# An attention kernel's last 64 keys as four 64 by 64 products, with a new order of the work

## The chip, the cores and the metric

One program runs on one core of a Trainium2 chip. The metric is the device time of one execution in microseconds (us). The kernel before has a median of 964.04 us over three runs (960.63 to 966.95). One further execution was taken with the profiler.

## The reference

The program is three layers, one after the other, in float32: an attention with a threshold, a block that adds the real part of a two-dimensional Fourier transform and an MLP (2048 hidden channels), and a block that mixes tokens with two 576 by 576 matrices. The change concerns the first layer alone.

```
batch, n_heads, seq, head_dim = (4, 8, 576, 64)
scores = scale * np.matmul(q, k.transpose(0, 1, 3, 2))
thresh = np.max(scores, axis=-1, keepdims=True) - tau
scores = np.where(scores >= thresh, scores, -1000000000.0)
scores = scores - np.max(scores, axis=-1, keepdims=True)
attn = np.exp(scores)
attn = attn / (np.sum(attn, axis=-1, keepdims=True) + 1e-09)
return np.matmul(attn, v).astype(np.float32)
```

A sequence has 576 = 4 x 128 + 64 tokens. The last 64 keys are what the four full blocks of 128 leave over.

## The kernel before

**The work of the attention.** The 32 heads are taken as 16 pairs `p` (0 to 15); `h` is 0 or 1, the head in its pair. The queries of a head are cut into two halves: half 0 has 256 queries, half 1 has 320. For every pair there are nine tiles of 128 queries. For each tile TensorE makes the scores in one bank pair `ps` (L454, L464, L469, L470), VectorE takes the maximum (`evac`, L478), ScalarE the exponential (`exp`, L483), VectorE multiplies by the mask and sums (`mask`, L494), TensorE transposes the result 128 by 128 (`turn`, L501, and L541 for the keys left over), and ScalarE copies the transposed blocks out of PSUM (`hi`, L510, L548, L550), to `st[h, half]` for the first 512 keys and to `st["r", h]` (tile `pt5`) for the last 64. In `st["r", h]` the queries of half 0 have their last 64 keys in partitions 0 to 63, and those of half 1 have theirs in partitions 64 to 127.

**The product with V** (`pv_ops`, L560, with its matmul at L571) is one operation `("pv", (p, half))` of the planner for each half. It takes a PSUM bank `O`, and for each of five blocks `kt` of 128 rows it issues one matmul for each head: V's block is the 128 by 64 weight, the transposed scores are the 256 or 320 columns that stream, and the heads write partitions 0 to 63 and 64 to 127 of the same bank. In the trace each of these float32 calls is two LDWEIGHTS and two MATMUL, so an operation `pv` is 20 of each. The fifth block holds the last 64 keys: V's block 4 has them in rows 0 to 63 with zeros below, and block 5 has zeros above and the same keys in rows 64 to 127; half 0 uses block 4, and half 1 block 5. Half of the rows of the fifth block are so multiplied by zero.

**After the product** VectorE multiplies each bank `O` by the reciprocal sums `R` into `xT` (L576): `("mu", p)` for half 0, after `pv` of half 0, then `("mul", p)` for half 1, after `pv` of half 1 and after `mu`. The bank is free again after that. GpSimd's first folding of the Fourier transform (`f0`, L675) waits for `mul`.

**The banks.** The tag `O` has four PSUM banks. They serve the transposes `T`, the spread of `R` (L611, L613), the products `O`, and the matmuls of the Fourier transform and the MLP.

**The order** is made when the program is built. Class `Plan` holds all operations with an engine, a cost, a priority, what they come after, and the buffers that they make and use. `schedule` runs a list schedule with these costs; `emit` issues the instructions in that order, so that each engine's order is fixed in the program. A long table `SHIFT` adds a number to the priority of each operation that fits a pattern, as `(('pv', 6), 26.31)`. The work of later layers (normalisation of finished rows, transposes `uT`, hidden layer `h` at L1194, output `acc` at L1214 to L1216, and so on) is in the same plan, so that it fills gaps of the attention.

Of the kernel before, what the change touches and what calls it, by code (L numbers as in the profile page):

```python
# [18 lines left out]
B, H, S, D = 4, 8, 576, 64  # L19
# [248 lines left out]
def attention_and_fft(pl, tc, ident, tb, pss, left, middle, right, qk, vv, cfk, cst, csr, u_d):  # L268
# [156 lines left out]
    def pair(p):  # L425
# [134 lines left out]
        def pv_ops(half, g):  # L560

            loc = {}
            a, n = ((0, 256), (256, 320))[half]
            b, j = divmod(heads(p), 4)

            def mms(e):
                O = loc["O"] = pl.bank([128, 512], f"O{p}_{half}")
                for kt in range(5):
                    for h in range(2):
                        w, x = VR[p][:, h * 6 + (kt if kt < 4 else 4 + half)], st[h, half][:, kt] if kt < 4 else st["r", h][:, :n]  # L570
                        e.matmul(O[64 * h:64 * h + 64, :n], w, x, start=(kt == 0), stop=(kt == 4))  # L571

            def mul(e):
                if p % 4 == 0 and not half:
                    xTs[b] = new("xT", [128, 4, S], f"xT{b}")
                e.tensor_mul(xTs[b][:, j, a:a + n], loc["O"][:, :n], st["R"][:, a:a + n])  # L576

# [4 lines left out]
            pl.op(("pv", k), "PE", 5 * TWO_PASS * n / 256 + 250, pr(g, 3), mms, deps + [("vr", p)], [O],  # L582
                  [("vr", p), ("pt5", p, 0), ("pt5", p, 1), (f"p0{half}", p), (f"p1{half}", p)])
            after = [("pv", k), ("Rc", p, half)] + ([("mu", p)] if half else []) + ([("mul", 4 * b)] if p % 4 else [])
# [385 lines left out]
THREE = 36  # L970
WARM = 7
# [607 lines left out]
class Late:  # L1579
# [180 lines left out]
    (('a6', 12), -9.79), (('a6', 4), -12.89), (('bound',), -9.54), (('bound', 11, 4), -148.11), (('bound', 12), 8.27),  # L1760
    (('bound', 12, 4), -142.12), (('bound', 13, 7), 18.02), (('bound', 13, 8), -21.26), (('bound', 14, 4), -258.91),
    (('bound', 3, 0), -117.73), (('bound', 3, 2), -273.97), (('bound', 6, 5), -179.47), (('bound', 6, 6), -259.98),
# [4 lines left out]
    (('evac', 2, 2), 163.27), (('evac', 3, 8), -187.58), (('evac', None, 3), 39.3), (('exp',), -39.47),  # L1767
    (('exp', 0), -196.98), (('exp', 0, 0), -8.7), (('exp', 0, 3), 56.52), (('exp', 0, 6), 230.59),
    (('exp', 0, 7), 2.61), (('exp', 1), -112.02), (('exp', 1, 5), 26.07), (('exp', 13, 3), 4.13),
    (('exp', 2, 6), 81.45), (('exp', None, 3), -32.63), (('exp', None, 6), -30.61), (('f', 0, 0, 2), -35.3),  # L1770
# [237 lines left out]
```

## Time and profile before

| what | value |
|---|---|
| median of three runs | 964.04 us (960.63 to 966.95) |
| profiled execution, its own time | 962.4 us |
| profiled execution, its span (first to last instruction) | 960.5 us |
| TensorE's matmuls busy | 937.9 us |
| VectorE busy | 626.9 us |
| ScalarE busy | 441.7 us |
| GpSimd busy | 301.9 us |
| granted clock of TensorE | 1.00 throughout |

The page calls TensorE's matmuls PE and its weight loads PEld, VectorE DVE, ScalarE ACT, GpSimd POOL. "Busy" is time in which at least one instruction of the engine is under way. Matmuls overlap in the pipeline, so that the sum of their durations is more than the time that they take; what one costs is read from the distance between starts. Attention fills about the first 330 us; the MLP and the token mixing come after it.

### The profile page before, as it was taken

The page shows a single profiled execution, that of the slowest core. Times are in us where ns is not written, and L with a number is a line of the kernel's source. Part 1 is how long each engine was busy: PE and PEld are TensorE (multiplying, and loading weights), DVE is VectorE, ACT ScalarE, POOL GpSimd, SP SyncE. Part 2 cuts the span into 40 slices and gives each one's busy share as a digit, 9 for nine tenths or more (in the row PEclk, how much of TensorE's full clock was granted, in tenths as well). Part 3 has the DMA queues.
Part 4 walks back from the last instruction along what each step waited for, and adds up shares of the span by engine and source line. Part 5 has one row for each costly group of instructions (what it writes and reads, how often), then busy time and mean ns, then how long its engine had stood idle before and what let it go on. Part 6 is the DMA issues. An engine that isn't in the chain of part 4 may idle for free.

```text
span 960.5 us, 15977 instructions
## 1 busy us (share of the span) xinstructions
PE 937.9 (98%) x5746; PEld 807.1 (84%) x5746; DVE 626.9 (65%) x1225; ACT 441.7 (46%) x835; POOL 301.9 (31%) x468
## 2 busy tenths in 40 slices
PE   8899999999999999999999999999999999999998
PEld 6666788788778788888888888999988899999998
DVE  6777888898898889963553255232257475486832
ACT  6777877787777645530332132011143242253500
POOL 3466656657664643520232032000000021130100
PEclk9999999999999999999999999999999999999999
DMA  6897747765772478645893575241518612213011
GB/s 180 217 218 177 192 122 189 188 187 123 230 188 63 148 221 239 193 132 127 227 291 131 118 218 187 67 86 46 164 30 302 180 41 66 53 56 91 23 51 50
DMA packets 136623, 139.53 MB, mean 145 GB/s; under 512 B 77536, under 2 KB 98720, under 8 KB 136160
## 3 DMA queue, kind: packets, MB, share of 16 engines
q1 hardware_dynamic: 135520, 134.87, 50.9%
q0 software_dynamic: 720, 2.76, 1.1%
q8 instruction: 46, 0.75, 0.3%
q10 hardware_dynamic: 304, 0.87, 0.3%
q14 instruction: 33, 0.27, 0.1%
HBM read 77.34 MB, written 32.05 MB: 114 GB/s over the span
## 4 chain that ended last, share of the span: by engine, by line
PE 80%; DVE 5%; ACT 3%; DMA 2%; issue 1%; SPq 0%; DVEq 0%; POOL 0%
PE h L1194 20%; PE y L1474 12%; PE acc L1216 7%; PE acc L1214 7%; PE acc L1215 7%; PE f L1539 5%; PE th L1351 5%; PE O L571 5%; PE T L501 3%; PE ps L469 2%; PE ps L470 2%; DVE P L494 1%; DVE c L478 1%; ACT P L483 1%; PE ps L464 1%
## 5 line engine op out<-in xcount | busy, mean ns | idle before, releaser
L1194 PE MATMUL h<-uh,w 128*128 128x512 f32 (+1 forms) x640 | 197.5, 370 | 0.1
L1199 ACT ACTIVATE hh<-h 128x512 fp32r<-128x512 f32 (+1 forms) x80 | 44.4, 555 | 222.4 <-PE acc L1215 166.3
L1203 DVE SCALAR_TENSOR_TENSOR hl<-h,hh 128x512 fp32r<-128x512 f32 (+1 forms) x80 | 50.7, 634 | 135.9 <-ACT hh L1199 135.8
L1194 PEld LDWEIGHTS h<-uh,w 128*128 128x128 f32 x640 | 118.8, 188 | 17.3 <-DVE hl L1203 0.2
L494 DVE SCALAR_TENSOR_TENSOR P<-ps,c,P 128x576 f32<-128x576 f32 x144 | 115.1, 813 | 11.7 <-ACT P L483 9.2
L478 DVE TENSOR_REDUCE c<-ps 128x1 f32<-128x576 f32 x144 | 106.1, 750 | 21.1 <-PE ps L470 13.4
L1194 PE MATMUL h<-ul,w 128*128 128x512 f32 (+1 forms) x320 | 118.1, 369 | 0.0
L483 ACT ACTIVATE P<-ps,c 128x576 f32<-128x576 f32 x144 | 105.9, 749 | 22.5 <-DVE c L478 19.1
L1214 PE MATMUL acc<-w,hh 128*128 128x512 f32 x288 | 112.8, 392 | 0.0
L1216 PE MATMUL acc<-w,hl 128*128 128x512 f32 x288 | 112.6, 391 | 0.0
L1215 PE MATMUL acc<-w,hh 128*128 128x512 f32 x288 | 112.4, 390 | 0.0
L1474 PE MATMUL y<-w,z 128*128 128x288 f32 x768 | 106.9, 294 | 0.0
L1474 PEld LDWEIGHTS y<-w,z 128*128 128x128 f32 x768 | 104.0, 188 | 0.9
L501 PE MATMUL T<-ident,P 128*128 128x128 f32 x576 | 83.7, 275 | 4.6 <-DVE P L494 2.0
L510 ACT COPY pt<-T 128x512 f32<-128x512 f32 (+1 forms) x160 | 83.8, 555 | 9.1 <-PE T L501 8.2
L571 PE MATMUL O<-pt,vr 128*64 128x256 f32 (+1 forms) x640 | 84.7, 411 | 0.5 <-ACT R L624 0.5
L469 PE MATMUL ps<-H,L 128*128 128x288 f32 x240 | 75.7, 332 | 3.7 <-DVE P L494 3.0
L501 PEld LDWEIGHTS T<-ident,P 128*128 128x128 f32 x576 | 66.7, 140 | 11.7 <-ACT pt L510 4.5
L571 PEld LDWEIGHTS O<-pt,vr 128*64 128x64 f32 x640 | 43.1, 137 | 31.2 <-issue 3.9
L1194 PEld LDWEIGHTS h<-ul,w 128*128 128x128 f32 x320 | 60.1, 188 | 8.9
L470 PE MATMUL ps<-X,L 128*128 128x288 f32 x240 | 67.0, 295 | 0.0
L1216 PEld LDWEIGHTS acc<-w,hl 128*128 128x128 f32 x288 | 54.1, 188 | 11.8
(358 smaller groups left out, 1678.5 us busy)
## 6 DMA issues: line engine op xcount, KB each, us to landing
raw<-in_qk SPq DMA_DIRECT2D x14, 608.0 KB
vr<-in_vv SPq DMA_DIRECT2D x16, 384.0 KB
w<-w_d SPq DMA_DIRECT2D x6, 992.0 KB
H<-hs SPq DMA_DIRECT2D x30, 160.0 KB
X<-raw SPq DMA_DIRECT2D x30, 160.0 KB
X<-hs SPq DMA_DIRECT2D x30, 160.0 KB
H<-raw SPq DMA_DIRECT2D x30, 160.0 KB
mu<-u_d SPq DMA_DIRECT2D x18, 256.0 KB
```

The lines of the kernel that those rows point to most:

```text
L469: e.matmul(ps[:, half, :HS], L[:, qo:qo + 128], H[:, ko:ko + HS], start=(j == 0), stop=False)
L470: e.matmul(ps[:, half, :HS], L[:, qo:qo + 128], X[:, ko:ko + HS], start=False, stop=(j == n - 1))
L478: e.tensor_reduce(loc["c4"][:, 0:1], loc["ps"][:, :, :HS], axis=AXES.XY, op=ALU.max, negate=True)
L483: e.activation(halves(), loc["ps"][:, :, :HS], AF.Exp, bias=loc["c4"][:, 0:1], scale=1.0)
L494: e.scalar_tensor_tensor(halves(), loc["ps"][:, :, :HS], loc["c4"][:, 1:2], halves(), op0=ALU.is_ge, op1=ALU.mult, accum_out=st["sums"][:, ...
L501: e.transpose(T[:, kt * 128:(kt + 1) * 128], P[:, kt * 128:(kt + 1) * 128], ident[:])
L571: e.matmul(O[64 * h:64 * h + 64, :n], w, x, start=(kt == 0), stop=(kt == 4))
L1194: e.matmul(loc["ps"][:, :n], a, x[:, c, :n], start=(k == 0), stop=(k == 11))
L1214: e.matmul(a, hh[:, q], wh, start=(f == 0), stop=False)
L1215: e.matmul(a, hh[:, q], wl, start=False, stop=False)
L1216: e.matmul(a, hl[:, q], wh, start=False, stop=(f == NF - 1))
L1474: e.matmul(loc["ps"][:, half, :HS], z[:, cs], w, start=(n == 0 and m == 0), stop=(n == 8 and m == 2))
```

## The change

For pairs 4 to 15 (`CORNERS_FROM = 4`) the operation `pv` of each half has only the four full blocks. When half 1 has issued its four, it issues `corners`: four matmuls with 64 rows and 64 weight columns each, two for each half and head, over the 64 partitions that hold the keys, without the zeros. The first two use rows 0 to 63 with output partitions 0 to 63 (half 0, head 0) and rows 64 to 127 with partitions 64 to 127 (half 1, head 1); the next two are head 0 of half 1 and head 1 of half 0. Outputs of half 0 go to the bank of half 0, those of half 1 to the bank of half 1.

From this follow other waits. `pv` of half 0 no longer waits for the copies of the last keys (`hi` with "r"). `pv` of half 1 comes after `pv` of half 0 and uses its bank too. `mu` comes after `pv` of half 1 instead of half 0, so that the bank of half 0 stays taken until then. Pairs 0 to 3 are as before. The planner's costs of `pv` change with it. The branch `MERGED` is off.

The last part of `SHIFT` (about 100 lines of numbers) is replaced by another, so the order of the operations on all engines is a new one.

```diff
+            crossed = p >= CORNERS_FROM
+            both = crossed and MERGED
+            def block(e, kt, half, n):
+                for h in range(2):
+                    w, x = VR[p][:, h * 6 + (kt if kt < 4 else 4 + half)], st[h, half][:, kt] if kt < 4 else st["r", h][:, :n]
+                    e.matmul(st["O", half][64 * h:64 * h + 64, :n], w, x, start=(kt == 0), stop=(kt == 4))
+            def corners(e):
+                for flip in range(2):
+                    for h in range(2):
+                        half = h ^ flip
+                        n, r = (256, 320)[half], slice(64 * half, 64 * half + 64)
+                        e.matmul(st["O", half][64 * h:64 * h + 64, :n], VR[p][r, h * 6 + 4 + half], st["r", h][r, :n], start=False,
+                                 stop=True)
             def mms(e):
-                O = loc["O"] = pl.bank([128, 512], f"O{p}_{half}")
-                for kt in range(5):
-                    for h in range(2):
-                        w, x = VR[p][:, h * 6 + (kt if kt < 4 else 4 + half)], st[h, half][:, kt] if kt < 4 else st["r", h][:, :n]
-                        e.matmul(O[64 * h:64 * h + 64, :n], w, x, start=(kt == 0), stop=(kt == 4))
+                for i in range(2) if both else (half,):
+                    if not both or i:
+                        st["O", i] = pl.bank([128, 512], f"O{p}_{i}")
+                    for kt in range(4 if crossed else 5):
+                        block(e, kt, i, (256, 320)[i])
+                if crossed and half:
+                    corners(e)
...
+            elif crossed and not both:
+                deps = [d for d in deps if half or d[1][1] != "r"]
+                pl.op(("pv", k), "PE", 4 * TWO_PASS * n / 256 + 250 + half * 660, pr(g, 3), mms, deps + [("vr", p)] + [("pv", (p, 0))] * half, [O],
+                      [("vr", p)] + (pts + [("O", (p, 0))] if half else pts[2:]))
+            elif not both:
+                pl.op(("pv", k), "PE", 5 * TWO_PASS * n / 256 + 250, pr(g, 3), mms, deps + [("vr", p)], [O], [("vr", p)] + pts)
-            after = [("pv", k), ("Rc", p, half)] + ([("mu", p)] if half else []) + ([("mul", 4 * b)] if p % 4 else [])
+            after = [("pv", (p, 1) if crossed else k), ("Rc", p, half)] + ([("mu", p)] if half else []) + ([("mul", 4 * b)] if p % 4 else [])
...
+CORNERS_FROM = 4
+MERGED = False
...
-    ((('zh', 2), 10), 46.37), ((('zh', 2, 1),), -1.67), ((('zh', 3),), 30.91), ((('zl', 2, 1), 17), 51.65),
-    (('Rc',), -77.86), (('Rc', 11, 0), -92.43), (('Rc', None, 1), -93.24), (('Re', 0), -6.46), (('Rt',), -3.02),
...
+    (('Rc',), -93.67), (('Rc', None, 1), -46.21), (('Re',), -69.91), (('Rt',), -11.46), (('Rt', 0, 1), 200.1),
...
```

## Rows read from the trace of the kernel before

**Rows 1.** The page: busy us by engine (share of span) x instructions; granted clock in slices

```profile
PE 937.9 (98%) x5746; PEld 807.1 (84%) x5746; DVE 626.9 (65%) x1225; ACT 441.7 (46%) x835; POOL 301.9 (31%) x468
...
PEclk9999999999999999999999999999999999999999
```

**Rows 2.** Windows (A:B, length, busy us with counts by engine, clock, DMA share, GB/s)

```profile
0.00:96.00 96.00, 86.10 (x579) 64.59 (x580) 69.06 (x162) 70.21 (x138) 50.30 (x109) 1.00 0.80 198
96.00:288.00 192.00, 186.31 (x1461) 153.96 (x1461) 170.91 (x406) 151.33 (x317) 120.59 (x230) 1.00 0.68 177
288.00:336.00 48.00, 47.50 (x360) 40.04 (x356) 40.87 (x87) 31.47 (x65) 25.59 (x47) 1.00 0.32 106
336.00:840.00 504.00, 502.45 (x2544) 436.90 (x2544) 272.82 (x409) 150.70 (x236) 91.52 (x74) 1.00 0.52 148
840.00:960.50 120.50, 115.57 (x810) 111.60 (x809) 73.20 (x165) 37.98 (x82) 13.86 (x11) 1.00 0.18 54
```

**Rows 3.** Groups by line: the product with V (busy us, mean ns)

```profile
L571 PE MATMUL O<-pt,vr 128*64 128x256 f32 (+1 forms) x640 | 84.7, 411 | 0.5 <-ACT R L624 0.5
```

**Rows 4.** Timeline (start us, us, engine, line, what, count, [idle before]): V product, pair 9

```profile
200.81 2.38 PE L571 MATMUL O<-pt,vr 128*64 128x256 f32 x20
...
203.12 0.19 PEld L469 LDWEIGHTS ps<-H,L 128*128 128x128 f32 x1 [0.39 <-issue]
...
205.25 2.91 PE L571 MATMUL O<-pt,vr 128*64 128x320 f32 x20
```

**Rows 5.** Timeline, stretches of some 0.1 us in pair 9's half 0: instructions then under way

```profile
200.81 0.44 PE L571 MATMUL O<-pt,vr 128*64 128x256 f32 x2
...
201.08 0.14 PEld L571 LDWEIGHTS O<-pt,vr 128*64 128x64 f32 x2
...
201.29 0.14 PEld L571 LDWEIGHTS O<-pt,vr 128*64 128x64 f32 x2
```

**Rows 6.** Timeline, short stretches in pair 0: its products of 64 by 64

```profile
11.43 0.27 PE L501 MATMUL T<-ident,P 128*128 128x128 f32 x1
...
11.63 0.46 PE L454 MATMUL ps<-x 64*64 64x288 f32 x2
...
11.93 0.14 PEld L454 LDWEIGHTS ps<-x 64*64 64x64 f32 x2
...
12.17 0.14 PEld L454 LDWEIGHTS ps<-x 64*64 64x64 f32 x2
...
12.41 0.41 PE L454 MATMUL ps<-x 64*64 64x288 f32 x2
...
12.75 0.18 PEld L454 LDWEIGHTS ps<-x 64*128 64x128 f32 x1 [0.44 <-issue]
...
13.10 0.19 PEld L454 LDWEIGHTS ps<-x 64*128 64x128 f32 x1
```

**Rows 7.** Timeline, pair 6: transposes, their copies, the product with V, the multiplications

```profile
147.95 0.42 DVE L576 TENSOR_TENSOR xT<-O,R 128x256 f32<-128x256 f32 x1
...
148.44 0.60 PE L501 MATMUL T<-ident,P 128*128 128x128 f32 x4
...
149.08 0.65 ACT L510 COPY pt<-T 128x256 f32<-128x256 f32 x2
...
150.78 2.91 PE L571 MATMUL O<-pt,vr 128*64 128x320 f32 x20
...
153.74 0.49 DVE L576 TENSOR_TENSOR xT<-O,R 128x320 f32<-128x320 f32 x1 [1.64 <-PE O L571]
154.31 0.74 POOL L675 TENSOR_TENSOR gte<-xT 128x256 f32<-128x256 f32 x1 [2.80 <-DVE xT L576]
```

**Rows 8.** Waits of TensorE in 0 to 336 us: total us, times, longest

```profile
PE ps L469 <- DVE P L494: 3.0, 5, 1.3
PE T L501 <- DVE P L494: 2.0, 3, 1.1
PE T L541 <- DVE P L494: 1.8, 2, 1.2
PE ps L464 <- DVE P L494: 1.7, 1, 1.7
PE T L501 <- ACT pt L510: 1.5, 3, 0.8
```

More of the change, by code (lines that the diff above doesn't have):

```diff
@@ L575, in mul @@
                     xTs[b] = new("xT", [128, 4, S], f"xT{b}")
-                e.tensor_mul(xTs[b][:, j, a:a + n], loc["O"][:, :n], st["R"][:, a:a + n])
+                e.tensor_mul(xTs[b][:, j, a:a + n], st["O", half][:, :n], st["R"][:, a:a + n])
             k = (p, half)
@@ L581, in pv_ops @@
             deps = [("hi", (p, i)) for i in idxs] + [("hi", (p, "r", i)) for i in ((0, 1), (0, 1, 2))[half]]
-            pl.op(("pv", k), "PE", 5 * TWO_PASS * n / 256 + 250, pr(g, 3), mms, deps + [("vr", p)], [O],
-                  [("vr", p), ("pt5", p, 0), ("pt5", p, 1), (f"p0{half}", p), (f"p1{half}", p)])
-            after = [("pv", k), ("Rc", p, half)] + ([("mu", p)] if half else []) + ([("mul", 4 * b)] if p % 4 else [])
+            pts = [("pt5", p, 0), ("pt5", p, 1), (f"p0{half}", p), (f"p1{half}", p)]
+            if both and half:
+                deps = sorted(set(deps + [("hi", (p, i)) for i in range(9)]), key=str)
+                pl.op(("ob", p), None, 0, pr(g, 3), hold, deps + [("vr", p)], [("O", (p, 0))])
+                pl.op(("pv", k), "PE", 4 * TWO_PASS * 576 / 256 + 540 + 380, pr(g, 3), mms, [("ob", p)],
+                      [O], [("O", (p, 0)), ("vr", p)] + pts + [(f"p00", p), (f"p10", p)])
+            elif crossed and not both:
[5 more added lines that the diff above has]
+            after = [("pv", (p, 1) if crossed else k), ("Rc", p, half)] + ([("mu", p)] if half else []) + ([("mul", 4 * b)] if p % 4 else [])
             made = [xT] if p % 4 == 0 and not half else []
@@ L1823 @@
-    (('turn', 6, 'r', 2), 30.33), (('turn', 7, 0), 52.88), (('turn', 7, 6), -48.38), (('turn', 8, 1), -6.83),
-    (('turn', 8, 5), -6.33), (('turn', 8, 'r', 0), 53.41), (('turn', 8, 'r', 2), -18.89), (('turn', 9, 3), 36.09),
-    (('turn', 9, 5), 873.6), (('turn', 9, 'r', 2), 5.09), (('turn', None, 0), -10.96), (('turn', None, 3), 1.46),
-    (('turn', None, 6), 1.04), (('turn', None, None, 0), -9.37), (('turn', None, None, 2), 5.29),
[6 rows of a table removed]
[25 rows of a table added]
+    (('a7',), -12.78), (('bound',), -95.59), (('bound', 11), 28.14), (('bound', 11, 7), 57.59), (('bound', 12), 8.27),
@@ new lines @@
+    (('bound', 13, 3), 44.69), (('bound', 2, 0), 65.87), (('bound', 8, 5), 215.69), (('bound', 9, 7), 127.98),
[5 rows of a table added]
+    (('evac',), -178.51), (('evac', 13), 19.4), (('evac', 2, 2), 163.27), (('evac', 3, 8), -187.58),
+    (('evac', None, 2), 18.13), (('exp',), -38.8), (('exp', 0), -207.81), (('exp', 0, 0), -8.7),
+    (('exp', 0, 3), 61.61), (('exp', 0, 6), 371.63), (('exp', 0, 7), 2.61), (('exp', 1), -109.89),
+    (('exp', 1, 5), 9.65), (('exp', 2, 1), 115.23), (('exp', 2, 6), 81.45), (('exp', 3, 1), 106.15),
[26 rows of a table added]
@@ new lines @@
+    (('mask',), -270.06), (('mask', 12, 7), 378.09), (('mix',), 25.77), (('mix', 0), -19.35), (('mix', 0, 3), -16.37),
+    (('mix', 0, 3, (0, 1), 0), -49.31), (('mix', 1, 0, (0, 1), 1), 57.12), (('mix', 1, 1, (0, 1), 0), -48.46),
+    (('mix', 1, 2, (0, 1), 0), 24.31), (('mix', 1, None, (0, 1)), 35.27), (('mix', 2), 8.04), (('mix', 2, 0), 34.55),
+    (('mix', 2, 1, (0, 1), 0), -48.26), (('mix', 2, 3), 10.11), (('mix', 2, 3, (0, 1), 0), -62.26),
+    (('mix', 2, 3, (0, 1), 7), -51.56), (('mix', 2, None, (0, 1)), 0.27), (('mix', 3), -36.8),
@@ new lines @@
+    (('mix', 3, 0, (1,), 0), 10.84), (('mix', 3, 2, (0,), 2), 72.52), (('mix', 3, 3), -25.32),
+    (('mix', 3, 3, (0,), 4), 123.76), (('mix', 3, None, (0,)), -18.45), (('mix', None, 0, (0,)), 16.78),
+    (('mix', None, 1), 17.12), (('mix', None, 2), -4.3), (('mix', None, 3, (0, 1)), -18.42),
+    (('mix', None, None, (0, 1)), -6.92), (('mix', None, None, (0, 1), 7), 16.69), (('n0',), 67.33),
[4 rows of a table added]
+    (('pv', None, 1), -1.05), (('raw', 14), 887.04), (('reload',), -0.55), (('second',), 143.83),
+    (('second', 4, 6), -140.9), (('ta',), 16), (('ta', 0), 126.78), (('ta', 15), 38.24), (('ta', 17), 90.07),
@@ new lines @@
+    (('table',), -55.5), (('th',), -21.67), (('th', 2), 10.47), (('th', 5), 5.29), (('th', 6), -0.27),
+    (('tl', 11), 42.06), (('tl', 4), 12.02), (('turn',), -0.34), (('turn', 0), -18.25), (('turn', 0, 0), -63.36),
+    (('turn', 0, 2), -102.19), (('turn', 0, 4), -57.47), (('turn', 0, 8), -26.78), (('turn', 1, 1), -43.85),
+    (('turn', 1, 2), -36.2), (('turn', 1, 'r'), -36.55), (('turn', 1, 'r', 0), 64.88), (('turn', 10, 1), -4.31),
+    (('turn', 10, 3), 17.42), (('turn', 10, 'r', 0), 57.47), (('turn', 11, 0), 32.88), (('turn', 11, 4), 29.86),
@@ new lines @@
+    (('turn', 11, 7), -12.81), (('turn', 12), -4.13), (('turn', 12, 1), -12.29), (('turn', 12, 2), -11.65),
+    (('turn', 12, 3), -5.86), (('turn', 12, 4), 18.88), (('turn', 13, 1), -6.02), (('turn', 13, 2), -21.03),
+    (('turn', 13, 4), 16.4), (('turn', 14), 5), (('turn', 14, 2), 15.41), (('turn', 14, 4), 86.51),
+    (('turn', 14, 'r', 0), 84.02), (('turn', 14, 'r', 2), -27.4), (('turn', 15), 15.62), (('turn', 15, 1), 23.18),
+    (('turn', 15, 2), -19.98), (('turn', 15, 4), 46.89), (('turn', 15, 5), 14.35), (('turn', 15, 7), 34.76),
@@ new lines @@
+    (('turn', 15, None, 0), 2.69), (('turn', 15, 'r'), -36.16), (('turn', 15, 'r', 0), 76.64), (('turn', 2), -4.2),
+    (('turn', 2, 2), -5.61), (('turn', 2, 4), 22.52), (('turn', 2, 5), -6.85), (('turn', 2, 6), 10.8),
+    (('turn', 2, 7), -12.55), (('turn', 2, 8), -1.75), (('turn', 2, 'r', 1), 28.6), (('turn', 2, 'r', 2), -21.23),
+    (('turn', 3), -4.45), (('turn', 3, 3), -4.8), (('turn', 3, 5), -2.89), (('turn', 3, 6), 11.7),
+    (('turn', 3, 7), -39.86), (('turn', 3, 8), 19.38), (('turn', 4, 0), 37.63), (('turn', 4, 7), 29.21),
@@ new lines @@
+    (('turn', 5), 0.92), (('turn', 5, 4), 19.48), (('turn', 5, 'r', 0), 59.05), (('turn', 6, 0), 29.53),
+    (('turn', 6, 1), -9.5), (('turn', 6, 4), 34.86), (('turn', 6, 'r', 2), 43.41), (('turn', 7), -2.89),
+    (('turn', 7, 'r'), -2.43), (('turn', 7, 'r', 0), 59.27), (('turn', 7, 'r', 2), -22.03), (('turn', 8), -0.66),
+    (('turn', 8, 0), 37.35), (('turn', 8, 2), -0.6), (('turn', 8, 4), 23.81), (('turn', 8, 5), -6.33),
+    (('turn', 8, 'r'), 1.43), (('turn', 8, 'r', 0), 60.36), (('turn', 8, 'r', 2), -17.65), (('turn', 9), 8.16),
@@ L1833 @@
+    (('turn', 9, 0), 25.84), (('turn', 9, 4), 34.61), (('turn', None, 0), -18.09), (('turn', None, 2), 1.31),
+    (('turn', None, 3), 1.74), (('turn', None, 4), -0.9), (('turn', None, 6), -0.35), (('turn', None, 7), -9.28),
+    (('turn', None, None, 0), -11.54), (('turn', None, 'r'), 6.95), (('turn', None, 'r', 0), -5.56),
[4 rows of a table added]
 )
```

32 lines of the change are left out of this document (2 added, 30 removed), and 120 rows, old and new, of the table SHIFT.

## The prediction

> **What bounds the kernel now.** I read the page first. TensorE has a matmul under way for 937.9 of the 960.5 us of the span, at a granted clock of 1.0, so at the upper of its two levels, 2.4 GHz; VectorE is next with 626.9 us [rows 1]. An average can mislead, so the table of windows comes second [rows 2]. From 336 to 840 us TensorE idles 1.6 us in 504. From 840 us on it idles 4.9 us. In the attention it idles 9.9 us before 96 us, 5.7 us from 96 to 288 us and 0.5 us from 288 to 336 us: 16.1 us in all. Pairs 4 to 15, the ones that change, lie in the last two of these stretches. There TensorE is busy for 97 and 99%, VectorE for 170.9 of 192 us (89%) and 40.9 of 48 us (85%). So TensorE bounds the stretch that changes, with VectorE not far behind. Since TensorE hardly idles from there to 840 us, and later layers' work fills gaps of the attention, I take time saved on TensorE in these pairs to arrive at the end one for one, unless it turns into waiting.
>
> Third, the waits of TensorE: the long ones are for VectorE's mask (L494), 8.5 us in the four rows that name it, and for ScalarE's copies, 1.5 us [rows 8]. No row on the product with V is among them. Last, the product itself: 640 matmuls, 84.7 us busy [rows 3]. In pair 9 half 0 takes 2.38 us and half 1 takes 2.91 us [rows 4]; sixteen times both is 84.6 us, so pair 9 stands for all.
>
> **The change, part by part.**
>
> *Removed: the fifth block of both halves.* A call is two matmul instructions, a block two calls, so a block is four of an operation's twenty instructions. In half 0 two matmuls are already under way in the first stretch, and two weight loads go together at 201.08 and again at 201.29: two matmuls run side by side, one for each head, in steps of 0.21 to 0.22 us (the ten steps of 2.38 us with the last one's drain) [rows 4, 5]. I take 0.215 us. Half 1 is 0.53 us longer over ten steps, so its step is 0.053 us longer: 0.27 us. A block is two steps: 0.43 us in half 0 and 0.54 us in half 1, 0.97 us for each pair.
>
> *Added: four products of 64 by 64.* Eight instructions. Two have 256 columns and two have 320, and a product of 320 cannot take less than its own two steps, 0.54 us. No row shows four at once. The nearest are pair 0's products of 64 by 64: two heads, on other rows and other columns, together, a step every 0.24 us (11.93 to 12.17, 12.17 to 12.41) for 288 columns [rows 6]; and the product with V, two heads on the same rows with other columns, together [rows 5]. The new case is two products on the same columns with other rows. Each writes its own bank there (half 0's or half 1's), so nothing that they write is shared. Below: 0.54 us, all four together. Above: 2 x (0.43 + 0.54) = 1.94 us, one after another; two by two it is 4 x 0.27 = 1.08 us. I take 0.54 us, because both kinds of neighbour in the trace run together, and the second does so although its products read the same rows.
>
> *Added: one change of shape.* The array goes from 128 rows by 64 columns to 64 by 64. Pair 0 shows what such a change costs. The last transpose before its 64 by 64 products starts at 11.43, and a transpose step is 0.11 us (four in 0.60 us, the last lasting 0.27 us) [rows 6, 7]; it has streamed by 11.54, and the next product starts at 11.63: 0.09 us. Its first step, 11.63 to 11.93, is 0.30 us instead of 0.24: 0.06 us. Together 0.15 us, taken. On the way out the last step starts at 12.41 and streams to 12.65, the next weights begin at 12.75, and the step after lasts 0.35 us instead of 0.24: 0.21 us, the upper end. The lower end is nothing, if a change between two narrow shapes costs less than these. The change back to full width is paid today too, after the fifth block: the weight loads are idle 0.39 us there and 0.44 us after pair 0's 64 by 64 [rows 4, 6]. I change nothing for it.
>
> *Sum for a pair.* 0.54 + 0.15 - 0.97 = -0.28 us. Twelve pairs: -3.4 us. With the shape change at its ends the twelve give -5.2 to -2.6 us.
>
> *Moved: the multiplication of half 0.* It now waits for half 1. In pair 6 it ran at 147.95, before half 1's product (150.78), and will run near 153.7, where the multiplication of half 1 now starts [rows 7]. Behind it on VectorE is the multiplication of half 1, which so ends up to 0.42 us later, and GpSimd's folding (L675) waits for that; GpSimd is busy 120.6 of 192 us [rows 2, 7]. Masks come behind both, but VectorE has 21 us free in those 192. I cost it at nothing; without this cover it is 0.42 us on VectorE's path for each pair, 5 us in all. The bank of half 0 stays taken up to 5.8 us longer (147.95 to 153.74); that is rival B.
>
> *Removed: half 0's wait for the last keys' copies.* TensorE's listed waits name no product with V [rows 8]: worth nothing. In return half 1 waits for half 0, which came first in pair 9 anyway [rows 4].
>
> *The new order.* It reaches every engine and can't be costed by rows. It can give back part of TensorE's 16.1 us of idling in the attention, or add to it; the amount of work stays the same. I take zero, with 3 us either way as an estimate, about a fifth of that idle time.
>
> The profiled execution took 962.4 us for a span of 960.5 us; minus 3.4 us makes 959.0 us. The median is 1.6 us higher, and from there it is 964.0 - 3.4 = 960.6 us.
>
> **The rivals.**
>
> A (the other side): the four products don't run side by side, because two of them share columns. Two by two, a pair pays 1.08 + 0.15 - 0.97 = +0.26 us, twelve +3.1 us: 967 us. All in a row it is +1.12 us, twelve +13.4 us: 977 us. It decides where `corners` takes more than 0.97 - 0.15 = 0.82 us. For it: no row shows shared columns. Against it: rows 5 show shared rows at no price.
>
> A': the instructions start strictly in the order of the program, so that a product's first instruction starts no earlier than the second one of the product before it. With 0.215 and 0.27 us steps the fourth product's second instruction then ends at 1.18 us, a pair pays +0.36 us, twelve +4.3 us: 968 us. Against it: by the same order half 0's first stretch would have one matmul under way, and has two [rows 5]. The Trainium skill states this order (TensorE: Matmul & The Clock Gate, Part 3: Packing small matmuls): matmuls are strict FIFO at start and at end, and only weight loads are pulled ahead. By that rule it would be 968 us, by the row 960.6 us; the trace does not agree with the rule for matmuls on different columns, so it has a small chance.
>
> B: banks. With both `O` banks held until half 1 is done, two of four are left for transposes. A transpose holds one from 148.44 until its copy ends near 149.73, 1.3 us [rows 7]: one in 0.65 us instead of the 0.44 us that four steps of 0.11 take. At one tile in about 1.5 us (0.44 us and the eight score matmuls) some four tiles fall into the 5.8 us, each 0.21 us late: 0.84 us for a pair, twelve times (0.84 - 0.28) is +6.7 us: 971 us. Against it: two banks suffice at one tile in 1.5 us, if tiles come evenly.
>
> C: no change. VectorE at 85 to 89% takes over as the bound, and the 0.28 us become waits for the mask, which already leads the waits [rows 2, 8]: 964 us.
>
> D: the new order is better. If half of the 16.1 us go, the sum is -11.4 us: 952.6 us. Against it: 9.9 of them lie in the first 96 us, where the DMA queues are 80% busy [rows 2] and the pairs don't change.
>
> **How the numbers follow.** Forecast 0.48, with 3 us of order either way 957 to 964 us. A and A' together 0.14 (of that 0.03 all in a row), B 0.10, C 0.14, D 0.14 (of that 0.09 beyond 1%). 1% is 9.6 us, about what a measurement of this kernel can tell from no change. Faster by over 1% (below 954.4 us) 0.09; slower by over 1% (above 973.7 us) 0.05: A in a row and some of B; the same 0.86. The range leaves out A in a row, the upper part of B and the better half of D: 952 to 969 us.
>
> **What would show it.** In the profile after, the product with V should fall from 84.7 us busy to between 79 and 82 us (twelve times 0.43 us less, or 0.28 us with the change of shape in it); four of the eight 64 by 64 matmuls should start within some hundredths of a us, and the next four 0.27 us later. Steps of 64 by 64 at two a time show A, one alone at first A'. New waits of transposes for L576 or L510 show B, more waiting for L494 shows C, less idle before 96 us shows D. It is wrong if TensorE's idle time before 336 us moves by more than its busy time does.

## The result and the profile after

The changed kernel has a median of 970.24 us (968.24 to 974.14, 9 runs), the kernel before, run beside it, 961.31 us (958.07 to 968.31, 9 runs). The ratio is 1.0087, with a 95% interval of 1.0058 to 1.0117. The forecast was 960.6 us and a range of 952 to 969 us, so the kernel became slower, by 8.9 us, where 3.4 us of gain were expected. The profiled execution took 974.1 us, the slowest of the nine, with a span of 972.3 us.

The page of the kernel after, busy time by engine and the granted clock in slices, to be held against [rows 1]:

```profile
PE 943.3 (97%) x5746; PEld 807.3 (83%) x5746; DVE 630.9 (65%) x1238; ACT 444.3 (46%) x837; POOL 285.7 (29%) x453
...
PEclk8899999999999989999999999999999999999999
```

TensorE has as many instructions as before. It idles 972.3 - 943.3 = 29.0 us instead of 22.6, and its busy time rose by 5.4 us although the product with V became shorter. The reason for the second stands in the last line: the clock was not full in three slices. Two of these slices are the first 48 us, ahead of the first product that changes. The clock does not explain the loss as a whole: two of the nine executions had a granted clock of 0.999 and 1.000 over their span, and they still took 969.35 and 968.24 us, 0.9 and 2.0 us less than the median. The kernel before took 957.2 to 964.0 us at such a clock in the later series.

Windows of the kernel after (columns as in [rows 2]):

```profile
0.00:96.00 96.00, 86.35 (x556) 63.95 (x557) 66.27 (x157) 66.88 (x131) 46.45 (x97) 0.93 0.79 194
96.00:288.00 192.00, 183.75 (x1445) 150.00 (x1443) 167.52 (x400) 155.13 (x321) 120.62 (x237) 1.00 0.67 175
288.00:336.00 48.00, 47.31 (x368) 38.03 (x366) 40.05 (x89) 32.57 (x68) 19.42 (x42) 1.00 0.38 113
336.00:840.00 504.00, 497.53 (x2492) 431.56 (x2491) 276.64 (x418) 147.09 (x230) 81.82 (x65) 0.99 0.52 149
840.00:972.30 132.30, 128.35 (x893) 123.75 (x891) 80.42 (x178) 42.64 (x89) 17.41 (x13) 0.99 0.16 50
```

Two stretches lose. From 96 to 288 us TensorE idles 8.25 us instead of 5.69, and from 336 to 840 us 6.47 us instead of 1.55. All of the latter lies just behind the attention. These are TensorE's waits from 326 to 440 us there, with total us, times, longest:

```profile
PE acc L1247 <- DVE hl L1234: 2.3, 2, 1.2
PE Xe L804 <- ACT ghe L741: 2.1, 1, 2.1
PE h L1225 <- DVE hl L1234: 2.1, 1, 2.1
PE acc L1245 <- ACT hh L1230: 0.7, 1, 0.7
```

In the kernel before the same list, from 336 to 432 us, holds 0.6 us. `hl` is the low part of the first hidden block of the MLP, which VectorE makes. `ghe` is ScalarE's rounded copy of the folded even rows of the last pairs, the first operand of the token transform; the folding itself is VectorE's work. Both stand behind the last multiplication.

**The products themselves came out as forecast.** Groups by line of the kernel after, the four full blocks and the corners, which answer to [rows 3]:

```profile
L570 PE MATMUL O<-pt,vr 128*64 128x256 f32 (+1 forms) x544 | 74.2, 417 | 0.5 <-ACT R L653 0.5
...
L577 PE MATMUL O<-pt,vr 64*64 64x256 f32 (+1 forms) x96 | 9.2, 428 | 0.0
```

The timeline of the kernel after in stretches of a few ns to 50 ns, in pair 15: what was under way in each (a group has the name of its first form):

```profile
330.07 0.44 PE L570 MATMUL O<-pt,vr 128*64 128x320 f32 x2
330.44 0.43 PE L577 MATMUL O<-pt,vr 64*64 64x256 f32 x1
...
330.44 0.49 PE L577 MATMUL O<-pt,vr 64*64 64x256 f32 x4
...
330.44 0.66 PE L577 MATMUL O<-pt,vr 64*64 64x256 f32 x6
...
330.44 0.76 PE L577 MATMUL O<-pt,vr 64*64 64x256 f32 x8
...
331.13 0.32 PE L642 MATMUL R<-ident,rr 128*128 128x128 f32 x1
```

One is under way at 330.44, four at 330.47, six at 330.73, eight at 330.78: the first instructions of all four products start within 0.03 us, and the second ones 0.27 to 0.33 us after the first. The last step of the full blocks starts at 330.07 and would end its 0.27 us at 330.34; the first corner comes at 330.44, so the change of shape costs 0.10 us. From the corners' last start (330.77) to the next work (331.13) it is 0.36 us, and the distance behind the fifth block is 0.36 us in the kernel before too. Half 1 so takes 0.10 + 0.33 - 0.27 = 0.16 us more than with its fifth block, and half 0 saves 0.43 us: -0.27 us for a pair, where -0.28 was forecast.

### The profile page after: what moved, and what is told of

The parts are those of the page before. It is cut to its first block, busy times and chain, and to the rows that moved or that the text cites. A ratio compares the mean times of both kernels' runs of the same rounds, so it can differ in the third digit from the quotient of the medians.

```text
span 972.3 us, 15986 instructions
## 1 busy us (share of the span) xinstructions
PE 943.3 (97%) x5746; PEld 807.3 (83%) x5746; DVE 630.9 (65%) x1238; ACT 444.3 (46%) x837; POOL 285.7 (29%) x453
## 4 chain that ended last, share of the span: by engine, by line
PE 74%; DVE 7%; DMA 3%; ACT 3%; issue 2%; SPq 1%; POOL 1%; DVEq 0%; ACTq 0%; POOLq 0%
PE h L1225 18%; PE y L1505 12%; PE acc L1247 6%; PE acc L1245 6%; PE acc L1246 6%; PE f L1570 5%; PE th L1382 5%; PE O L570 4%; PE T L501 3%; PE ps L469 2%; PE ps L470 2%; ACT P L483 1%; DMA u_d<-u 1%; DVE c L478 1%; DVE P L494 1%
## 5 line engine op out<-in xcount | busy, mean ns | idle before, releaser
L501 PE MATMUL T<-ident,P 128*128 128x128 f32 x576 | 86.7, 280 | 3.9 <-DVE P L494 2.2
L570 PE MATMUL O<-pt,vr 128*64 128x256 f32 (+1 forms) x544 | 74.2, 417 | 0.5 <-ACT R L653 0.5
L1245 PEld LDWEIGHTS acc<-w,hh 128*128 128x128 f32 x288 | 54.1, 188 | 11.5 <-ACT hh L1230 1.1
```

The lines of the kernel that those rows point to most:

```text
L501: e.transpose(T[:, kt * 128:(kt + 1) * 128], P[:, kt * 128:(kt + 1) * 128], ident[:])
L570: e.matmul(st["O", half][64 * h:64 * h + 64, :n], w, x, start=(kt == 0), stop=(kt == 4))
L1245: e.matmul(a, hh[:, q], wh, start=(f == 0), stop=False)
```

## The experiments

Each was run beside the kernel before; ratios are to it, with 95% intervals. Two parts had to be told apart first: the products and the new order.

### The corners in the order of before

The old table of priorities, eleven pairs with corners (not pair 6, where its order leaves no bank free if both of half 0 and half 1 stay taken). Where the old order has the multiplication of half 0 (`mu`) ahead of half 1's product, it goes right behind that product; elsewhere it stays where it is in VectorE's queue.

```diff
-                for kt in range(5):
+                for kt in range(4 if crossed else 5):
...
+                if crossed and ("O", 1 - half) in st:
+                    corners(e)
...
+CROSSED = (4, 5, 7, 8, 9, 10, 11, 12, 13, 14, 15)
+MOVED = (5, 8, 14)
```

> The order of the kernel before, kept operation by operation, with the four 64 by 64 products in place of the fifth blocks in 11 of the 12 pairs (not in pair 6, where both banks held at once leave none free); half 0's multiplication moves a few places, right behind half 1's product, in pairs 5, 8 and 14, and stays where it was in the others. Theory O (the new order loses the time, the products gain it): eleven times -0.28 us = -3.0 us, ratio to the kernel before 0.997 (0.993 to 1.001). Theory S (the products' own waits lose it: both banks held, half 0's multiplication late): slower than before, by up to the +8.9 us of the changed kernel, ratio 1.005 to 1.01. A clock theory (TensorE's clock drops whenever the last 64 keys are issued as narrow products): low clock in the profile and a ratio above 1.

Measured: 978.12 us, 1.0173 (1.0137 to 1.021). VectorE's waits from 96 to 336 us in this kernel (total us, times, longest):

```profile
DVE xT L620 <- PE O L605: 19.2, 9, 3.2
```

The row of before that answers to it has 4.0 us in five waits. What that does to the masks, in VectorE's timeline of the same kernel (start, us, ..., idle before):

```profile
111.95 0.42 DVE L620 TENSOR_TENSOR xT<-O,R 128x256 f32<-128x256 f32 x1 [2.30 <-PE O L605]
...
112.42 0.81 DVE L526 SCALAR_TENSOR_TENSOR P<-ps,c,P 128x576 f32<-128x576 f32 x1
...
113.15 0.81 DVE L526 SCALAR_TENSOR_TENSOR P<-ps,c,P 128x576 f32<-128x576 f32 x1
```

`mu` stands ahead of two masks and waits 2.30 us for the corners; the masks wait behind it, and TensorE's next transposes and scores for them. So the multiplication's new wait is free only if `mu` stands in VectorE's queue where its product is already done. The prediction saw the masks behind `mu`, and still costed the wait at nothing because VectorE has free time.

### The same with both multiplications together, and that move alone

`mu` goes directly ahead of `mul` in all eleven pairs, with the corners (first kernel) and with the old five blocks (second).

```diff
+        for p in MOVED:
+            mu = at["mu", p]
+            order.remove(mu)
+            order.insert(order.index(at["mul", p]), mu)
...
+MOVED = (4, 5, 7, 8, 9, 10, 11, 12, 13, 14, 15)
```

> As the run old_order_corners (order of the kernel before, four products in 11 pairs, not in pair 6), but half 0's multiplication stands directly ahead of half 1's in all 11 pairs, behind the masks that VectorE has there. In old_order_corners it stood ahead of them, and VectorE waited 2.3 us for half 1's product with the masks queued behind. Theory O (the changed kernel's new order is its loss; the products gain 0.28 us for each pair): eleven times -0.28 = -3.0 us, ratio 0.997 (0.993 to 1.001). Theory S (multiplying half 0 late and holding two banks costs more than the products give, wherever it stands): ratio above 1.003, with TensorE idling more than the 22.6 us of before.

> The order of the kernel before with half 0's multiplication directly ahead of half 1's in the same 11 pairs, and all five blocks of 128 rows as before: no narrow product. Theory O: nothing happens, ratio 1.000 (0.997 to 1.003), and the difference to old_order_mul_together is the products' 3.0 us. Theory S: slower by what the late multiplication costs, ratio 1.003 to 1.015.

Measured: with corners 958.61 us, 0.9975 (0.9955 to 0.9994); the move alone 960.87 us, 1.0000 (0.9983 to 1.0017). So the late multiplication, with the bank kept for it, costs nothing that can be measured here. The corners bring 2.3 us by the medians, 0.2 us for each of the eleven pairs, though the two intervals overlap a little. This version beats both kernels: it is 0.25% faster than the one before and some 1.3% faster than the changed one (0.9975 against the 1.0104 below).

### The new order without the corners, and the changed kernel again

The changed kernel's order, waits and late `mu`, but with the fifth blocks of 128 rows where it has the corners; beside it the changed kernel itself.

```diff
-                    corners(e)
+                    block(e, 4, 0, 256)
+                    block(e, 4, 1, 320)
```

> The changed kernel with its order, its waits and its late multiplication, but the two fifth blocks of 128 rows in place of the four products, issued at the same place. Theory O: the order's loss stays and the gain goes: twelve times +0.28 us = +3.3 us on the changed kernel, about +12 us on the kernel before, ratio 1.012. If the gain of the products never reached the end in this order (it turns into waiting), the time is that of the changed kernel, ratio 1.009. If the products themselves were the loss, it would fall back towards 1.000.

> The changed kernel once more, beside the other two on one chip: ratio 1.009 by its first measurement. By the clock theory its profile shows low clock again in the first 32 us and near 342 and 356 us; if the low clock of the first profile was a matter of one execution, this profile has the same waits on TensorE after 334 us (about 5 us of idling to 345 us) with less of it.

Measured: 971.78 us, 1.0123 (1.0097 to 1.015), and 969.79 us, 1.0104 (1.0075 to 1.0133). The corners gain about 2 us in this order too, though the intervals overlap. Without them the new order is 1.2% slower than the old one (1.0123 against the 1.0000 of the late move alone). The whole loss belongs to the order.

**Where the order loses.** The changed kernel's second profile and the profile of both multiplications together hold the same TensorE work but for one pair. First the page and three windows of the changed kernel (span 966.3 us), then of the other (span 956.2 us):

```profile
PE 938.3 (97%) x5746; PEld 803.2 (83%) x5746; DVE 632.8 (65%) x1238; ACT 444.1 (46%) x837; POOL 284.2 (29%) x453
...
96.00:288.00 192.00, 183.96 (x1448) 149.84 (x1450) 167.44 (x398) 153.59 (x320) 116.16 (x229) 1.00 0.68 174
...
336.00:432.00 96.00, 91.51 (x436) 75.59 (x437) 85.34 (x103) 44.15 (x59) 39.43 (x25) 0.98 0.65 199
...
336.00:360.00 24.00, 20.95 (x120) 18.50 (x121) 21.12 (x32) 11.80 (x19) 6.99 (x4) 0.93 0.56 167
```

```profile
PE 934.8 (98%) x5746; PEld 803.2 (84%) x5746; DVE 625.1 (65%) x1225; ACT 442.6 (46%) x835; POOL 303.5 (32%) x468
...
96.00:288.00 192.00, 186.32 (x1468) 151.80 (x1469) 170.94 (x407) 150.64 (x316) 120.33 (x228) 1.00 0.68 176
...
336.00:432.00 96.00, 95.95 (x455) 79.94 (x455) 82.20 (x101) 44.80 (x57) 42.33 (x26) 1.00 0.64 194
...
336.00:360.00 24.00, 23.95 (x139) 20.93 (x139) 22.02 (x32) 12.11 (x18) 11.08 (x8) 1.00 0.79 238
```

The spans differ by 10.1 us: 6.6 us of TensorE idling (28.0 against 21.4) and 3.5 us of busy time. Of the idling 2.4 us are from 96 to 288 us and 4.4 us from 336 to 432 us. The busy time is clock: 0.93 in 24 us means that 3.4 of them ran at 1.2 GHz, and the window from 24 to 48 us, also at 0.93, has as much. Each costs half of that, 1.7 us. The earlier of the two is no mark of the new order: the profile of the late move alone, in the old order, has 0.93 in the same window.

What TensorE waits for from 96 to 288 us can be read as well. For masks it is 3.9 us in the changed kernel's second profile and 3.9 us in the kernel before. What is new are waits for VectorE's steps of the Fourier transform, which the lists of the kernel before and of the fast old order do not have:

```profile
PE uT L1157 <- DVE dm L887: 0.8, 1, 0.8
PE R L642 <- DVE u L865: 0.7, 1, 0.7
```

Three more of this kind make 1.3 us. `uT` and `R` do not read `dm` or `u`. By the program these steps empty a bank of the tag `O`, so part of this may be a wait for a bank. No run takes it apart.

### One order for the attention, the other behind it

The new order up to the last pair's `mul` and the old one behind it (with the changed kernel's products), and the reverse: the old order with both multiplications together up to there, the new one behind.

```diff
+        cut = order.index(self.names["mul", NP - 1]) + 1
+        head = order[:cut]
+        for name, e in OTHER:
+            i = self.names[name]
+            if i not in done:
+                head.append(i)
+                self.ran[i] = e
```

> The changed kernel's order up to the last pair's multiplication (about the first 330 us), and from there what is left in the order of the kernel before. The changed kernel idles on TensorE 19.0 us in its first 336 us (kernel before 16.1 us) and 6.5 us from 336 to 432 us (before 0.7 us). Theory T (the loss sits behind the attention, where the last pair's folding meets the weight blocks): most of the 8.9 us comes back, ratio 0.998 to 1.003. Theory M (the loss sits in the attention's order): ratio 1.006 to 1.010. Half and half: 1.004 to 1.006, plus what the seam costs, because the two orders have done different work of the later layers by then.

> The other way round: the order of old_order_mul_together (0.9975 of before, with the products in 11 pairs) up to the last pair's multiplication, then what is left in the order of the changed kernel. Theory T: slower by most of the loss, ratio 1.003 to 1.008, with TensorE idling 4 to 7 us between 336 and 432 us and its clock low there. Theory M: ratio 0.997 to 1.000, TensorE idling there about as before (0.7 us).

(In its first 336 us the changed kernel's TensorE idles 18.6 us in the first profile and 19.6 in the second, not 19.0.) Measured: 968.75 us, 1.0074 (1.0053 to 1.0094), and 965.95 us, 1.0048 (1.0023 to 1.0073). Against the 0.9975 of the old order with corners the kernel with the new attention loses 1.0% and the one with the new rest 0.7%; both together, as in the changed kernel, 1.3%. The two don't add up, and each hybrid has a seam of its own at 326 to 345 us. TensorE's wait for `hl` there, first with the new attention, then with the new rest:

```profile
PE acc L4675 <- DVE hl L4662: 4.6, 2, 2.7
```

```profile
PE acc L4690 <- DVE hl L4677: 4.7, 2, 4.1
```

So replacing one half of the new order by the old brings back a part of the loss at most (the first interval overlaps with that of the changed kernel). How much each half loses by itself is not shown, since the seam may be a large part of either number.

### Five edits of the new order behind the attention

In the changed kernel the last pair's chain on VectorE is slow. VectorE's timeline of the kernel after, from the last multiplication to the low part of the even rows (`gle`), an operand of the token transform:

```profile
331.95 0.49 DVE L595 TENSOR_TENSOR xT<-O,R 128x320 f32<-128x320 f32 x1 [0.19 <-ACT R L653]
332.36 1.22 DVE L1069 SCALAR_TENSOR_TENSOR raw('w', 2)_4804<-raw('w', 2)_4804 128x1024 int32<-128x1024 int32 x1
333.49 2.14 DVE L704 TENSOR_TENSOR gte<-xT 128x256 f32<-128x256 f32 x1
335.55 0.41 DVE L704 TENSOR_TENSOR gto<-xT 128x256 f32<-128x256 f32 x1
...
338.25 1.51 DVE L1069 SCALAR_TENSOR_TENSOR raw('w', 1)_4803<-raw('w', 1)_4803 128x1024 int32<-128x1024 int32 x1
339.68 2.15 DVE L735 TENSOR_TENSOR ge<-ge,ge 128x289 f32<-128x289 f32 x1
342.33 0.46 DVE L745 TENSOR_TENSOR gle<-ge,ghe 128x289 fp32r<-128x289 f32 x1 [0.50 <-ACT ghe L741]
```

The same chain in the kernel before:

```profile
326.81 0.49 DVE L576 TENSOR_TENSOR xT<-O,R 128x320 f32<-128x320 f32 x1
327.44 1.26 DVE L1038 SCALAR_TENSOR_TENSOR raw('w', 1)_4766<-raw('w', 1)_4766 128x1024 int32<-128x1024 int32 x1
328.63 0.41 DVE L675 TENSOR_TENSOR gte<-xT 128x256 f32<-128x256 f32 x1
...
332.07 0.67 DVE L716 TENSOR_TENSOR gle<-ge,ghe 128x289 fp32r<-128x289 f32 x1
```

From the multiplication's end to `gle` it is 4.8 us before (327.30 to 332.07) and 9.9 us after (332.44 to 342.33). Three things differ: in the kernel before GpSimd does the middle steps of that folding, VectorE has two steps on the MLP's weights in the chain (L1069) where it had one (L1038), and two foldings take 2.1 us where their like take 0.41 and 0.45. The kernel before has such a slow folding too, on the odd rows (2.16 us from 332.66, beside GpSimd's sign step), and TensorE hardly waits for it (0.6 us).

**The collision.** In the first edit GpSimd's sign steps on weight blocks 1 and 3 wait until the even folding is done (a small copy of its result is put ahead of them), and VectorE's next step on block 1 goes directly behind that folding.

```diff
+                if key in (("w", 1), ("w", 3)):
+                    e.tensor_copy(pl.hold[:, :2], FOLDED[0][:, :2])
```

> The changed kernel with one thing moved: GpSimd's sign steps for weight blocks 1 and 3 (1024 columns each, 2 to 3 us) wait until VectorE has folded the even rows of the last pair. In the changed kernel's profile these steps run beside VectorE's folding, which takes 2.14 and 2.15 us where it takes 0.41 and 0.45 us alone, and TensorE then waits 2.07 us for it and its clock falls for 3.4 us. Theory P (this collision makes the loss between 334 and 360 us): the two foldings are short, TensorE's 2.07 us go, about 3 to 5 us less than the changed kernel, ratio to before 1.005 to 1.007. If what follows is late anyway (the weights of block 1 come later, so that the hidden layer waits instead): same as the changed kernel, ratio 1.009 to 1.010.

Measured: 972.86 us, 1.0127 (1.0104 to 1.015). The foldings became short, but TensorE now waits for `gle`, `hl`, `glo` and `xle`, 7.7 us in all from 336 to 432 us. The edit made a wait of its own, in VectorE's timeline:

```profile
335.84 1.49 DVE L1082 SCALAR_TENSOR_TENSOR raw('w', 1)_4804<-raw('w', 1)_4804 128x1024 int32<-128x1024 int32 x1 [2.19 <-POOL raw('w', 1)_4804 L1079]
```

VectorE's step on block 1 waits 2.19 us for the delayed sign step, and `gle` stands behind it (337.26): the chain is still 8.6 us. It is the same trap as with `mu`. So this run shows that the collision can be taken away without a gain, not what the collision costs.

**The filler.** The kernel before keeps part of batch 2's Fourier work for TensorE behind the last product; the new order does most of it earlier. Two edits put four pieces of it (two groups `Y` and two transposes), or the two transposes alone, back behind the first hidden block.

```diff
+MOVES = (
+    (('Y', (2, 1), 'e'), ('first', (0, 0))),
+    (('Y', (2, 1), 'o'), ('hh', (0, 0))),
...
+    (('Ut', (2, 1), 1), ('Ua', (2, 1), 0)),
+)
```

> The changed kernel with one edit in its order: the last second-stage work of batch 2's Fourier transform (two matmul groups Y, two transposes uT and what depends on them), which it does before and beside pair 15's product with V, goes behind the first hidden block, where the kernel before has it. Theory F, that the loss behind the attention is missing filler for TensorE while the last pair is folded and transformed: TensorE's idle time from 336 to 432 us falls from 4.5 to 6.5 us in the changed kernel to under 3 us, and the ratio to the kernel before from 1.009 or 1.010 to 1.003 to 1.006; what remains is the order ahead of pair 15. Rival G, that the loss is spread over the whole order and the work is only missing elsewhere when it is moved back: idle time moves from 336 to 432 us to the stretch from 288 to 336 us, where pair 15's steps lose their cover, and the ratio stays between 1.008 and 1.012.

> The changed kernel with only the two transposes uT of batch 2's last part (first half of them behind the first hidden block, second half behind the first output block) moved back; the two matmul groups Y stay ahead of pair 15's product. Theory F: half of the gain of moving all of it, so a ratio of 1.006 to 1.008 and 1 to 2 us less idle time from 336 to 432 us than the changed kernel's 4.5 to 6.5 us. Rival G: 1.008 to 1.012 and no less idle time from 288 to 432 us in sum (5.2 us in the changed kernel's slower profile for 336 to 432 us with 0.7 us before that).

(The changed kernel's idle time in the slower profile, which the second one names, is 6.5 us from 336 to 432 us and 0.7 us before; their sum is 7.2 us, not 5.2.) Measured: 974.70 us, 1.0152 (1.0132 to 1.0172), and 973.99 us, 1.0139 (1.0123 to 1.0155). TensorE's first waits from 326 to 440 us with the four pieces moved:

```profile
PE Xe L844 <- ACT ghe L781: 5.9, 1, 5.9
PE acc L1300 <- DVE hl L1287: 2.4, 2, 2.0
```

More work for TensorE did not shorten the wait: its sums go through VectorE, ahead of the folding of the even rows, which so ends later (at 346.00).

**The chain.** The even folding goes straight through, VectorE's two weight steps and a copy behind it, GpSimd's sign step on block 1 as well.

```diff
+    (('c1', ('w', 1)), ('fl', (3, 'o', 0))),
+    (('c2', ('w', 2)), ('fl', (3, 'e', 0))),
+    (('hl', (0, 0)), ('g', (3, 'e', 0))),
...
```

> The changed kernel with one edit in its order: after pair 15's last multiplication VectorE does the even folding for the token transform straight through; its two steps on weight blocks 1 and 2 and a copy of batch 2, which stand between the foldings, and GpSimd's sign step on block 1 come behind the even folding. From the last multiplication's end to the first operand of the transform (ge's low half) the kernel before takes 4.8 us, the changed kernel 9.9 us in both of its profiles. Theory H, that this chain of 9.9 us on VectorE is what TensorE waits for behind the attention: the chain falls to 5 us or less, TensorE's idle time from 336 to 432 us falls from 4.5 to 6.5 us to under 3 us, no half clock near 340 us, and the ratio falls from 1.009 or 1.010 to 1.004 to 1.007. Rival I, that something is always late there, because the last pair's folding, the first hidden block and the weights all need VectorE in the same 10 us: the chain gets short, but TensorE then waits for weights, for the hidden block's low half or for the transform's results, and the ratio stays between 1.008 and 1.013.

Measured: 973.82 us, 1.013 (1.0099 to 1.016). The chain fell to 4.4 us (333.07 to 337.49). The first waits of the same list in this kernel:

```profile
PE Xo L844 <- DVE u L905: 3.6, 1, 3.6
PE Xo L844 <- DVE xle L863: 2.1, 1, 2.1
PE acc L1298 <- DVE hl L1285: 1.6, 1, 1.6
```

The wait is now for `u`, batch 2's sums, which this edit puts in VectorE's queue behind the odd rows' folding (`glo` ends there at 344.16, `u` at 344.88), and for the results of the even rows.

**The weights.** Loading and converting blocks 1 and 2 begins earlier, with the steps ahead of the last multiplication, as before.

```diff
+    (('c1', ('w', 2)), ('Re', 15)),
+    (('c2', ('w', 2)), ('wl', 0)),
+    (('c4', ('w', 2)), ('c2', ('w', 2))),
+    (('c1', ('w', 1)), ('c0', ('w', 1))),
...
```

> The changed kernel with one edit in its order: loading and converting the MLP's weight blocks 1 and 2 begins earlier, with both sign steps on GpSimd and three steps on VectorE ahead of pair 15's last multiplication, as the kernel before has them (there block 2's two steps start 4.2 and 2.9 us before that multiplication's end and block 1's first 0.1 us after it; in the changed kernel they start 0.1 us before, 12.1 us after and 5.8 us after); the hidden block's low half goes behind the even folding. Theory J, that the new order's loss behind the attention is this VectorE and GpSimd work put behind the last multiplication, where folding, hidden block and token transform all need VectorE: from the last multiplication's end to ge's low half 5 us or less (9.9 in the changed kernel, 4.8 before), TensorE's idle time from 336 to 432 us under 3 us instead of 4.5 to 6.5 us without more of it from 288 to 336 us, and a ratio of 1.004 to 1.007. Rival I, that VectorE has too little room on either side of that multiplication: the steps ahead of it make pair 15's masks or its multiplication late, idle time moves to 288 to 336 us, and the ratio stays between 1.008 and 1.013.

Measured: 974.32 us, 1.0146 (1.0118 to 1.0173). The chain is 4.7 us, but TensorE idles 4.0 us from 288 to 336 us (0.7 in the changed kernel's first profile, 1.9 in its second) and 6.8 us from 336 to 432 us:

```profile
PE h L1282 <- DVE hl L1291: 3.9, 1, 3.9
PE h L1282 <- DVE xT L635: 1.9, 1, 1.9
PE acc L1304 <- DVE hl L1291: 1.1, 1, 1.1
```

So five edits, each of which moved in the trace what it was to move, all gave 1.013 to 1.015, none of them less than the unedited new order (1.0087 and 1.0104; the intervals of some overlap with it). Folding, weights, hidden block and transform share VectorE in those 15 us, and in each of these five runs TensorE still waited there for its results, the old ones or others. None of the five moves wins, which is not to say that none of the five items has a part in the loss: the edits lengthened the old wait or put a new one in its place. Which moves in the new table cost the 12 us is not settled, nor was the part ahead of pair 15 (2.4 us of idling from 96 to 288 us) taken apart.

## Why the prediction was wrong

- **The forecast failed at one step, the new order.** It was taken as zero with 3 us either way, "about a fifth of that idle time". The runs give some 1.2%, about 12 us, with corners (1.0104 against 0.9975) and without (1.0123 against 1.0000). The estimate was drawn from TensorE's idle time in the attention. But idle time bounds only what an order can give back. What it can lose is bounded by nothing in that row. A better sign was in the windows: VectorE at 85 to 89% in the stretch that changes [rows 2], and a kernel whose TensorE idles 1.55 us in the 504 us behind it, so that a move there can hardly win. Against the kernel before in the same series (961.31 us, not the 964.04 us that the forecast starts from) the change was +8.9 us where -3.4 was forecast: the 12.3 us between them are about what the order costs. Why this order costs them is only in part known.
- **Removed and added work: right.** -0.27 us a pair in the trace against -0.28. The 0.15 us for the change of shape came out too: 0.10 us until the first corner starts, and 0.06 us more in the corners' first step (0.33 us from the first start to the last instead of 0.27). In the time of whole runs it came to some 2 us instead of 3.4, with noise of about that size.
- **Four products not side by side (A, A'): refuted.** All four start within 0.03 us. The Trainium skill (TensorE: Matmul & The Clock Gate, Part 3: Packing small matmuls) has matmuls start strictly in the order of the program. Here the second instruction of the first product starts some 0.25 us after the first one of the fourth, so the trace doesn't agree. Nor do the second instructions come in that order: the program has a product of 256 columns last, but from 330.72 to 330.75 both instructions of the two products of 256 columns are under way and only the first of each of 320.
- **Banks (B): not seen in the old order, open in the new.** The late move alone, which keeps half 0's bank until half 1 is done in eleven pairs, is 1.0000. In the new order `uT` and `R` wait 1.5 us for steps that they do not read, which may be for a bank (above).
- **Late multiplication at nothing: right only by position.** Behind the masks it cost nothing, ahead of them 17.8 us (978.12 against the 960.31 us of the kernel before beside it). The text named the masks as standing behind it, and trusted VectorE's free 21 us to cover the wait; in that run VectorE waited 19.2 us with the masks queued behind, so its free time covered nothing.
- **No change (C) and a better order (D): no.** The old order with corners is faster than before, so VectorE did not take the gain, and TensorE's waits for masks from 96 to 288 us are as long as before. The new order gave nothing back in sum: TensorE idles 29.0 us instead of 22.6.
- **The signs named in advance.** The product with V fell from 84.7 us to 82.5 us busy (74.2 and 9.2 with their overlap taken off), just above the 79 to 82 that were named; drained ends count in it, and starts give the better measure. The alarm named last, TensorE's idle time before 336 us, could tell nothing: in a fixed stretch idle and busy time add up to its length, so both move alike (2.5 us here). The larger loss, 4.9 us of idling from 336 to 840 us, lies where the prediction did not look.

## What to carry to other kernels

Cost a change of order by itself: let the local edit run in the old order, with the smallest move that it needs (here both multiplications together), before the order is made anew around it. An operation that gets a later input must also get a later place in its engine's queue, behind the work that does not wait. Where the bounding engine idles hardly at all, a new order has little to win; what it can lose is to be looked for in the queue of the second engine, here at the seam between two stages.

## What the hardware showed

- **Half clock behind waits.** The kernel before and the fast old order with corners have 1.00 from 336 to 360 us. The windows of that stretch in the kernel after and, below it, in the kernel with the straight folding:

```profile
336.00:360.00 24.00, 18.78 (x97) 16.05 (x96) 19.75 (x34) 9.29 (x16) 7.70 (x5) 0.86 0.53 147
```

```profile
336.00:360.00 24.00, 18.09 (x91) 15.38 (x92) 19.61 (x25) 9.05 (x17) 8.61 (x6) 0.79 0.38 112
```

  TensorE idled 5.2 and 5.9 us of those 24, and 0.86 and 0.79 mean that the clock was at 1.2 GHz for 6.7 and 10.1 us. That adds at most 3.4 and 5 us to the idling; where TensorE stood idle at half clock, it adds nothing. Not every wait is followed by it: the kernel with the early weights idled 4.0 us from 288 to 336 us at 1.00. And in a whole run it is the smaller part: the changed kernel's executions at 0.999 and 1.000 are 0.9 and 2.0 us below its median, which is 8.9 us above the kernel before.
- **VectorE beside GpSimd.** `gte` of 128 by 256 took 2.14 us from 333.49, where `gto`, of the same shape, took 0.41 us; GpSimd's sign step on 128 by 1024 ran from 333.19 for 2.15 us, and both end within 0.3 us of each other. The Trainium skill says that a VectorE instruction with two inputs in SBUF and a GpSimd one that reads SBUF contend, and that the order of issue decides which of them blocks (SBUF — State Buffer, Who interferes with whom); the rows agree, with `gte`, issued second, ending 0.29 us after the sign step.
- **Four quarters of the array together.** Products on shared rows and on shared columns, into two banks, cost little more than the longest of them: 0.33 us from the first start to the last, where a step of 320 columns alone is 0.27.
